# Attention and a gated feed-forward layer in one launch: low words on VectorE, leaky ReLU by one maximum, weights decoded during attention

## The chip, the cores and the metric

The kernel runs on one core of a Trainium2 chip. The metric is the device time of one execution in microseconds (us); the median of three runs before the change is 1651.07 us, the lowest 1649.44 and the highest 1653.55. The engines are TensorE (PE in the profile, its weight loads PEld), VectorE (DVE), ScalarE (ACT), GpSimd (POOL) and SyncE (SP), which issues the DMAs.

## The reference

First attention over 8 batches and 8 heads, 576 tokens, head width 64, in which scores more than `tau` under the row maximum are dropped; then a two-layer network with a leaky ReLU of one slope per hidden unit (512 to 2048 to 512, 4608 tokens). The inputs are float32 (the kernel reads the two weights as 64-bit words).

```python
scores = scale * np.matmul(q, k.transpose(0, 1, 3, 2))
thresh = np.max(scores, axis=-1, keepdims=True) - tau
scores = np.where(scores >= thresh, scores, -1000000000.0)
attn = np.exp(scores - max); attn = attn / (sum + 1e-09)
x = np.matmul(attn, v)            # then heads side by side: 4608 x 512
h = x @ w_in
g = np.maximum(h, 0.0) + alpha * np.minimum(h, 0.0)
return g @ w_out
```

## The kernel before

Matrix products are made in reduced float32 with operands split in a high word and a low word, `hi` rounded by ScalarE and `lo = value - hi` by a subtraction, and three matmuls per product: high by high, high by low, low by high.

The program has four stages. **Attention** runs over 32 pairs of heads, nine units each, one unit per cycle of the written order; functions are put at a cycle by `at_cycle(cycle, function)`, and each cycle issues what stands there on every engine in that order. A cycle is meant to last about 2.6 us. Between the units go the matmuls of the first 6 of 16 hidden blocks for all tokens, with the results kept in DRAM (`part`). TensorE makes scores (L424), VectorE the row maximum (L439) and the mask `p` (L459), ScalarE the exponential (L447).

**The left-over stage** finishes three groups of tokens (the jobs, tiles `phj`, `ptj`, `gj`, `accj`) by the same functions: `layer1_into` (L211), `prelu` (L229, L230), `split_g` (L238, L241), `layer2` (L247). Beside them `first_weights` decodes the first layer's ten other blocks, one every three cycles. A 64-bit word is taken apart by `Split64`: two operations on ScalarE (`size`: L134, L135), `clamp` (L138), then on VectorE `shift` (L141), `sign` (L146) and `power` (L151), then a product `rest` and a sum. `sums_at` makes from two blocks the seven weight operands of a fast 2x2 product with seven multiplications in place of eight, with high and low words (`wa`).

**The first product** has 30 units (six supers of 768 tokens by five pairs of blocks) of seven products each, each six matmuls of 384 columns (L1195), in the order `USE` = 1, 7, 2, 6, 4, 5, 3 into the banks X, W and Y. `after_a` (L1205 to L1227) makes the leaky ReLU: products 1, 7 and 6 are copied to SBUF by ScalarE (L1211); 2, 4 and 5 add the copy (VectorE, L1224), make the part under zero (L1225) and add the larger (L1226); product 3 takes VectorE (L1219), ScalarE (L1220) and POOL (L1221). `x_at` makes the next super's token operands, sums on POOL (`xt`, L1134 to L1144), `xh` on ScalarE (L842), `xl` on POOL (L845). The second layer's words are decoded in the same stage, one piece every 12 cycles (`word_at`; L826 and L830 are its sum and product).

**The second product** has nine groups of 512 tokens with seven products of 30 matmuls of 256 columns (L1353), in three parts with a cycle each. `gates_at` makes the operands: `gh` by ScalarE (L842), `gl` by VectorE for products 7 and 5 and by POOL for the other five (L845). Three pairs of buffers serve them in turn, so a product's `gh` waits until the product three before it is done. `after_b` adds the result into the output tile (L1369).

Of the kernel before, what the change touches and what calls it, by code (L numbers as in the profile page):

```python
# [79 lines left out]
def tile_masked_attention_moe(  # L80
# [31 lines left out]
    class Split64:  # L112
# [8 lines left out]
        def load(self):  # L121
            tag, bufs = self.raw_tag
            self.raw = self.pool.tile([P, DM], I64, tag=tag, name=f"wr{self.name}", bufs=bufs)
            nc.sync.dma_start(self.raw.rearrange("p (a b) -> p a b", a=self.a), self.src)

        def size(self):
# [4 lines left out]
            if pool is mem:  # L131
# [689 lines left out]
    def word_at(c, w, dst, load):  # L821


        def join():
            low, t = f(w.low), f(w.t)
            w.eng[2].tensor_tensor(dst, t, low, op=ALU.add)  # L826
# [6 lines left out]
        at_cycle(c, w.size)  # L833
# [5 lines left out]
        at_cycle(c + 6, join)  # L839
# [7 lines left out]
    def fetch_x(t0, n, c, lead, name):  # L847
# [24 lines left out]
        return st  # L872

    with tc.manual_schedule(engines=ENGINES) if ENGINES else ExitStack():
# [72 lines left out]
        def word_piece(io, fc):  # L947
            src = (src_i if io == "i" else src_o)(fc)
            return Split64(mem.ws, ("w0", 2), mem.ws, ("w1", 2), ENG2[(fc + (io == "o")) % 2], *src)

# [4 lines left out]

        def sums_at(c, pr):
# [97 lines left out]
        def second_layer(job, pool):  # L1054
            puts = []
            for o in range(0, job.n, P):
# [149 lines left out]
        def after_a(u, prod):  # L1206
            s, pr = divmod(u, NP)
            ph = bank[u, BANK[prod]][:, :H1]
            if prod in (1, 7, 6):
# [66 lines left out]
        def gates_at(s):  # L1276
# [179 lines left out]
```

## Time and profile before

| quantity | value |
|---|---|
| median of three runs | 1651.07 us |
| profiled execution | 1653.89 us |
| span of its trace | 1652.1 us |
| mean granted TensorE clock | 0.931 |
| TensorE matmuls busy | 1395.0 us (84%) |
| VectorE busy | 1228.5 us (74%) |
| ScalarE busy | 917.4 us (56%) |
| POOL busy | 884.8 us (54%) |

All rows come from one profiled execution. Busy time is that of the instructions that compute. [...] A wait is named by what released it last. The stages begin at 0, 836, 974 and 1294 us of the span, read from TensorE's instructions.

### The profile page before, as it was taken

Reading aid. Unit: us, or ns where it says so; the run is one execution under the profiler, and the core shown is the slowest. Engines: PE = TensorE matmul, PEld = TensorE weight load, DVE = VectorE, ACT = ScalarE, POOL = GpSimd, SP = SyncE. Lnnn points to the kernel's source line nnn. Section 1 sums busy time; section 2 is a strip of 40 time slices with the busy share of each in tenths; the row PEclk is TensorE's granted clock in tenths of the full one; section 3 lists DMA queues with packets and bytes.
Section 4 is the critical chain, followed back from the end, with each engine's and each line's share of the span. In section 5 each row is a group of like instructions: output and inputs, shape, how many; then the busy total and the mean of one; then the engine's idle time right before and its main releaser. Section 6 shows DMA issues by size and latency. Waiting matters only on the chain.

```text
span 1652.1 us, 26173 instructions
## 1 busy us (share of the span) xinstructions
PE 1395.0 (84%) x8998; PEld 1287.9 (78%) x8998; DVE 1228.5 (74%) x2203; ACT 917.4 (56%) x2019; POOL 884.8 (54%) x910
## 2 busy tenths in 40 slices
PE   6998999999999999999985577787787677777777
PEld 4667899998989999989975467786777677777777
DVE  7888889888898888888826788899889544444443
ACT  7888788888898888888733333332234222222222
POOL 4774656656576666666544445545655433333334
PEclk9998999999999999999988778999999788888889
DMA  7555454453554445545132333343324433333321
GB/s 221 162 147 138 108 142 132 138 159 110 144 143 129 139 126 147 139 133 149 45 95 74 102 106 112 134 145 118 107 84 166 154 125 114 118 121 115 104 67 52
DMA packets 143286, 205.08 MB, mean 124 GB/s; under 512 B 15696, under 2 KB 88688, under 8 KB 143152
## 3 DMA queue, kind: packets, MB, share of 16 engines
q1 hardware_dynamic: 143152, 203.39, 41.4%
q8 instruction: 72, 1.18, 0.3%
q14 instruction: 62, 0.51, 0.1%
HBM read 109.13 MB, written 52.05 MB: 98 GB/s over the span
## 4 chain that ended last, share of the span: by engine, by line
PE 57%; DVE 13%; issue 11%; ACT 8%; POOL 7%; DMA 4%; SPq 1%; ACTq 0%; POOLq 0%; DVEq 0%
PE av L571 10%; PE s L424 9%; PE acca L247 7%; PE pX L1353 7%; PE pha L211 7%; PE t L468 6%; POOL gl L845 4%; PE pX L1195 3%; PE pW L1353 3%; DVE ct L1225 3%; DMA wri<-in_moe_w_in_dram 2%; PE pY L1353 2%; DVE c L1224 2%; PE pW L1195 1%; ACT gh L842 1%
## 5 line engine op out<-in xcount | busy, mean ns | idle before, releaser
L439 DVE TENSOR_REDUCE nmx<-s 128x1 f32<-128x576 f32 x288 | 217.0, 754 | 79.0 <-PE s L424 75.4
L845 POOL TENSOR_TENSOR gl<-gr,gh 128x1280 fp32r<-128x1280 f32 x36 | 108.2, 3007 | 205.5 <-ACT gh L842 205.5
L1195 PE MATMUL pX<-xh,wa 128*128 128x384 f32 x480 | 147.9, 364 | 76.5 <-ACT c L1211 54.8
L459 DVE SCALAR_TENSOR_TENSOR p<-s,thr,p 128x576 f32<-128x576 f32 x256 | 206.9, 808 | 3.0 <-ACT thr L452 2.4
L447 ACT ACTIVATE p<-s,nmx 128x576 f32<-128x576 f32 x256 | 190.1, 742 | 5.9 <-DVE nmx L439 5.4
L424 PE MATMUL s<-kh,qst 128*128 128x288 f32 x640 | 145.0, 317 | 43.7 <-DVE p L459 28.2
L1353 PE MATMUL pX<-wb,gh 128*128 128x256 f32 x720 | 157.2, 319 | 20.7 <-ACT gh L842 20.7
L247 PE MATMUL acca<-wo,ga 128*128 128x512 f32 x540 | 169.1, 425 | 1.6 <-POOL ga L241 1.5
L1195 PEld LDWEIGHTS pX<-xh,wa 128*128 128x128 f32 x480 | 94.8, 202 | 88.2 <-ACT c L1211 61.3
L468 PE MATMUL t<-ident,p 128*128 128x128 f32 x1024 | 156.9, 277 | 0.0
L424 PEld LDWEIGHTS s<-kh,qst 128*128 128x128 f32 x640 | 101.7, 194 | 70.8 <-issue 39.3
L842 ACT ACTIVATE gh<-gr 128x1280 fp32r<-128x1280 f32 x45 | 55.9, 1262 | 179.0 <-issue 77.4
L1353 PEld LDWEIGHTS pX<-wb,gh 128*128 128x128 f32 x720 | 133.6, 227 | 23.9 <-ACT gh L842 23.9
L1353 PE MATMUL pX<-wb,gl 128*128 128x256 f32 x360 | 115.9, 322 | 39.5 <-POOL gl L845 39.5
L211 PE MATMUL pha<-xh,wi 128*128 128x256 f32 x720 | 146.5, 287 | 1.8 <-DVE tt L524 1.5
L424 PE MATMUL s<-kl,qst 128*128 128x288 f32 x640 | 135.1, 302 | 0.0
L468 PEld LDWEIGHTS t<-ident,p 128*128 128x128 f32 x1024 | 128.3, 143 | 0.2
L211 PEld LDWEIGHTS pha<-xh,wi 128*128 128x128 f32 x720 | 117.5, 190 | 7.0 <-DVE tt L524 2.4
L1353 PEld LDWEIGHTS pX<-wb,gl 128*128 128x128 f32 x360 | 82.0, 228 | 42.8 <-POOL gl L845 42.8
L571 PE MATMUL av<-eo,vst 128*128 128x322 f32 (+1 forms) x512 | 107.8, 334 | 0.0
L247 PEld LDWEIGHTS acca<-wo,ga 128*128 128x128 f32 x540 | 96.1, 194 | 13.9 <-POOL ga L241 2.0
L424 PEld LDWEIGHTS s<-kl,qst 128*128 128x128 f32 x640 | 104.1, 194 | 0.0
(201 smaller groups left out, 4079.9 us busy)
## 6 DMA issues: line engine op xcount, KB each, us to landing
gd<-c SPq DMA_DIRECT2D x90, 192.0 KB
gr<-gd SPq DMA_DIRECT2D x24, 640.0 KB
kr<-in_k_dram SPq DMA_DIRECT2D x31, 320.0 KB
rb<-rvd SPq DMA_DIRECT2D x64, 144.0 KB
xs<-xa SPq DMA_DIRECT2D x32, 288.0 KB
pin<-part SPq DMA_DIRECT2D x18, 512.0 KB
out_dram<-pin SPq DMA_DIRECT2D x18, 512.0 KB
vr<-in_v_dram SPq DMA_DIRECT2D x28, 320.0 KB
```

Of the source, the lines that this page charges most:

```text
L211: nc.tensor.matmul(ph[:, :n], w[:, c, :], xx[:, c, :n], start=(c == 0 and ti == 0), stop=(c == NCC - 1 and ti == 2),)
L247: nc.tensor.matmul(acc[:m, :], gg[:, g, o : o + m], w, start=(first and ti == 0), stop=(last and ti == 2))
L424: nc.tensor.matmul(ps[:, h, :288], w, kk[:, a + h * 288 : a + (h + 1) * 288], start=(ki == 0 and i == 0), stop=(ki == 1 and i == n - 1),)
L439: nc.vector.tensor_reduce(self.nmx[:, j : j + 1], self.S[u][0][:, :, :288], axis=AX.XY, op=ALU.max, negate=True)
L447: nc.scalar.activation(pj, ps[:, :, :288], AF.Exp, bias=nmx[:, j : j + 1], scale=1.0)
L459: nc.vector.scalar_tensor_tensor(pj, ps[:, :, :288], thr[:, j : j + 1], pj, op0=ALU.is_ge, op1=ALU.mult, accum_out=self.sm[:, c : c + 1])
L468: nc.tensor.transpose(tb[:, c, :], pt[:, j, j * D + c * P : j * D + (c + 1) * P], ident)
L571: nc.tensor.matmul(pa[:m, :n], w, x, start=(part == 0 and c == 0), stop=(part == z.parts[-1] and c == NKC))
L842: nc.scalar.activation(dst, src, AF.Copy)
L845: eng.tensor_tensor(dst, src, f(hi), op=ALU.subtract)
L1195: nc.tensor.matmul(ph[:, :H1], a, x[:, c], start=(fresh and c == 0 and ti == 0), stop=(c == 1 and ti == 2), skip_group_check=not fresh,)
L1353: nc.tensor.matmul(acc[:, tb * H2 : (tb + 1) * H2], g[:, pr, tb * P : (tb + 1) * P], w, start=(fresh and n == 0 and ti == 0), stop=(n == l ...
```

## The change

Three parts. **One:** the ten blocks' words of the first layer are decoded in attention, from cycle 62 on, one piece every 20 cycles, with clamp, product and sum on POOL, shift, sign and power on VectorE; the float32 result goes to DRAM (`wid`) and is read back after attention, so that `first_weights` holds only reads and sums, one pair every six cycles. **Two:** the leaky ReLU is one maximum: where alpha is at most 1 it is max(h, alpha h), and otherwise minus the maximum of -h and -alpha h; `signs` makes per hidden unit `turn` (1 or -1) and the products with it, the second layer's weights carry `turn`, and ScalarE's copies scale by it. The sum goes to PSUM (product 5 to a bank of its own, Z), ScalarE copies it to SBUF one cycle later, and one VectorE operation two cycles later makes the maximum. POOL's sum for product 3 goes. The second layer's words are decoded one piece every 14 cycles. **Three:** all `gl` of the second product are on VectorE.

```diff
+EW0, EW = 62, 20
+    def signs():
+        ts = nc.vector.tensor_scalar
+        ts(turn_sb, alpha_sb, 1.0, 2.0, op0=ALU.is_le, op1=ALU.mult)
+        ts(turn_sb, turn_sb, -1.0, None, op0=ALU.add)
+        ts(tiny_sb, turn_sb, 2.0**-52, None, op0=ALU.mult)
+        nc.vector.tensor_tensor(slope_sb, turn_sb, alpha_sb, op=ALU.mult)
+    wid = [dram.tile([P, DM], F32, name=f"wid{fc}") for fc in fcs2]
...
+    def early_word(n, c):
+        fc = fcs2[n]
+        w = Split64(mem, ("wx", 1), mem, ("wxt", 1), "ppp", *src_i(fc))
+        def done(w):
+            nc.gpsimd.tensor_tensor(f(w.t), f(w.t), f(w.low), op=ALU.add)
+            nc.sync.dma_start(wid[n], f(w.t))
+        word_at(c, w, c - 5, done)
...
+    at_cycle(6, signs)
+    for n_ in range(NJ):
+        early_word(n_, EW0 + EW * n_)
...
         def first_weights(c0, step):
-            for n, fc in enumerate(fcs2):
-                w = word_piece("i", fc)
-                c = c0 + step * n
-                at_cycle(c + 6, start_w32, fc)
-                word_at(c, w, None, c - 3)
...
+            for pr in range(NP):
+                c = c0 + step * pr
+                for r in range(2):
+                    at_cycle(max(i, c - 6), fetch_w32, 2 * pr + r)
+                sums_at(c, pr)
...
-        first_weights(i + 4, 3)
+        first_weights(i + 4, 6)
...
-                nc.scalar.activation(t, ph, AF.Copy)
+                nc.scalar.activation(t, ph, AF.Copy, scale=turn_sb[:, fc : fc + 1])
                 return
...
+            def larger(g, whole, slope):
+                stt(g, whole, slope[:, col], g, op0=ALU.mult, op1=ALU.max)
+                nc.sync.dma_start(gd[2 * s + k][r, pr], g)
             if of is None:
-                nc.vector.tensor_scalar(t, ph, 0.0, al, op0=ALU.min, op1=ALU.mult)
-                nc.scalar.activation(g, ph, AF.Relu)
-                nc.gpsimd.tensor_tensor(g, g, t, op=ALU.add)
+                copy(g, ph, scale=turn_sb[:, col])
+                at_cycle(i + 1, larger, g, ph, slope_sb)
             else:
                 g = sv.pop((u, of))
-                nc.vector.tensor_tensor(g, ph, g, op=ALU.add)
-                nc.vector.tensor_scalar(t, g, 0.0, al, op0=ALU.min, op1=ALU.mult)
-                nc.vector.scalar_tensor_tensor(g, g, 0.0, t, op0=ALU.max, op1=ALU.add)
+                whole = ph
+                if prod == 5:
+                    whole = ps_3.tile([P, 512], F32, tag="Z", name=f"pZ{u}")[:, :H1]
+                stt(whole, ph, turn_sb[:, col], g, op0=ALU.mult, op1=ALU.add)
+                at_cycle(i + 1, copy, g, whole)
+                at_cycle(i + 2, larger, g, whole, alpha_sb)
...
+            w = Split64(mem.ws, ("w0", 3), mem.ws, ("w1", 2), "ppp", *src_o(fc))
+            def done(w):
+                dst = wo32[:, n // 2, n % 2]
+                nc.vector.scalar_tensor_tensor(
+                    dst, f(w.t), turn_sb[:, fc : fc + 1], f(w.low), op0=ALU.mult, op1=ALU.add
+                )
+            word_at(c, w, c - 4, done, fc)
...
-            c = begin + 8 + 12 * n
+            late_word(n, begin + 8 + 14 * n)
...
-                split_lo(nc.vector if n in (7, 5) else nc.gpsimd, gop[s, n][1], st[src(n)], gop[s, n][0])
+                split_lo(nc.vector, gop[s, n][1], st[src(n)], gop[s, n][0])
```

On VectorE, in the first product, seven products of one unit: `c` are the tiles with the saved copies, `ct` temporary ones, `pX`, `pY`, `pW` PSUM banks. Before:

```order
L1224 TENSOR_TENSOR c_12_14008<-pY_14023,c_12_14008 128x384
L1225 TENSOR_SCALAR ct_12_14040<-c_12_14008,alpha_sb 128x384
L1226 SCALAR_TENSOR_TENSOR c_12_14008<-c_12_14008,ct_12_14040 128x384
L1219 TENSOR_SCALAR ct_11_14051<-pX_13900,alpha_sb 128x384
L1224 TENSOR_TENSOR c_12_14065<-pW_14010,c_12_14065 128x384
L1225 TENSOR_SCALAR ct_12_14074<-c_12_14065,alpha_sb 128x384
L1226 SCALAR_TENSOR_TENSOR c_12_14065<-c_12_14065,ct_12_14074 128x384
L1224 TENSOR_TENSOR c_12_14031<-pX_13978,c_12_14031 128x384
L1225 TENSOR_SCALAR ct_12_14094<-c_12_14031,alpha_sb 128x384
L1226 SCALAR_TENSOR_TENSOR c_12_14031<-c_12_14031,ct_12_14094 128x384
```

After:

```order
L1253 SCALAR_TENSOR_TENSOR pZ_13995<-pX_13882,turn_sb,c_11_13920 128x384
L1241 SCALAR_TENSOR_TENSOR c_11_13920<-pZ_13995,alpha_sb,c_11_13920 128x384
L1253 SCALAR_TENSOR_TENSOR pY_13997<-pY_13997,turn_sb,c_12_13982 128x384
L1241 SCALAR_TENSOR_TENSOR c_12_13982<-pY_13997,alpha_sb,c_12_13982 128x384
L1241 SCALAR_TENSOR_TENSOR cr_14022<-pX_13882,slope_sb,cr_14022 128x384
L1253 SCALAR_TENSOR_TENSOR pW_13985<-pW_13985,turn_sb,c_12_14035 128x384
L1241 SCALAR_TENSOR_TENSOR c_12_14035<-pW_13985,alpha_sb,c_12_14035 128x384
L1253 SCALAR_TENSOR_TENSOR pZ_14065<-pX_13956,turn_sb,c_12_14004 128x384
```

Three operations per product with two of them on SBUF alone have become two, both with a PSUM operand, and each maximum stands a product later than its sum.

On POOL, at a boundary of two supers: `xt` and `xr` are sums of token tiles, `xl` low words, `wo` and `wto` the second layer's words. Before:

```order
L1221 TENSOR_TENSOR cr_14131<-cr_14131,ct_12_14130 128x384
L1134 TENSOR_TENSOR xt_7_14167<-xr_11_13999,xr_01_14002 128x768
L845 TENSOR_TENSOR xl_1_14165<-xr_00_13997,xh_1_14164 128x768
L826 TENSOR_TENSOR wo_12979<-wto_14106,wro_14063 128x512
L845 TENSOR_TENSOR xl_7_14194<-xt_7_14167,xh_7_14193 128x768
L1141 TENSOR_TENSOR xt_6_14208<-xt_7_14167,xr_00_13997 128x768
L845 TENSOR_TENSOR xl_2_14206<-xr_10_14005,xh_2_14205 128x768
L1144 TENSOR_TENSOR xt_4_14224<-xr_10_14005,xt_6_14208 128x768
L1221 TENSOR_TENSOR cr_14227<-cr_14227,ct_13_14226 128x384
L845 TENSOR_TENSOR xl_6_14239<-xt_6_14208,xh_6_14238 128x768
```

After:

```order
L144 TENSOR_SCALAR wto_14074<-wto_14074 128x512
L1152 TENSOR_TENSOR xt_7_14131<-xr_11_13973,xr_01_13976 128x768
L843 TENSOR_TENSOR wro_14031<-wro_14031 128x512
L868 TENSOR_TENSOR xl_1_14129<-xr_00_13971,xh_1_14128 128x768
L868 TENSOR_TENSOR xl_7_14158<-xt_7_14131,xh_7_14157 128x768
L1159 TENSOR_TENSOR xt_6_14173<-xt_7_14131,xr_00_13971 128x768
L868 TENSOR_TENSOR xl_2_14171<-xr_10_13979,xh_2_14170 128x768
L1162 TENSOR_TENSOR xt_4_14185<-xr_10_13979,xt_6_14173 128x768
L868 TENSOR_TENSOR xl_6_14197<-xt_6_14173,xh_6_14196 128x768
L1156 TENSOR_TENSOR xr_01_13976<-xr_01_13976,xr_00_13971 128x768
```

The sums `cr` are gone; a clamp (`wto`, L144) and a product of words (`wro`, L843) stand there in place of the sum `wo`, and the order of the token operands is the same.

On VectorE, in the second product, some of one token group: `gt` and `gr` are sums of gates, `gl` the low words, `pin` the output tiles. Before:

```order
L845 TENSOR_TENSOR gl_5_16614<-gr_10_16190,gh_5_16613 128x1280
L1306 TENSOR_TENSOR gt_7_16627<-gr_00_16442,gr_10_16460 128x1280
L1369 TENSOR_TENSOR pin_1_16285<-pW_16444,pin_1_16285 128x2x256
L845 TENSOR_TENSOR gl_7_16652<-gt_7_16627,gh_7_16651 128x1280
L1369 TENSOR_TENSOR pin_0_16551<-pX_16638,pin_0_16551 128x2x256
L1317 TENSOR_TENSOR gr_01_16207<-gr_01_16207,gt_6_16474 128x1280
L1369 TENSOR_TENSOR pin_1_16285<-pX_16370,pin_1_16285 128x2x256
L1309 TENSOR_TENSOR gt_6_16743<-gr_11_16487,gt_7_16627 128x1280
L1369 TENSOR_TENSOR pin_1_16553<-pW_16713,pin_1_16553 128x2x256
L1369 TENSOR_TENSOR pin_0_16551<-pY_16759,pin_0_16551 128x2x256
L1369 TENSOR_TENSOR pin_0_16283<-pX_16370,pin_0_16283 128x2x256
```

After:

```order
L868 TENSOR_TENSOR gl_1_16759<-gr_00_16622,gh_1_16758 128x1280
L1407 TENSOR_TENSOR pin_1_16465<-pX_16550,pin_1_16465 128x2x256
L868 TENSOR_TENSOR gl_5_16796<-gr_10_16372,gh_5_16795 128x1280
L1344 TENSOR_TENSOR gt_7_16809<-gr_00_16622,gr_10_16641 128x1280
L1407 TENSOR_TENSOR pin_1_16465<-pW_16625,pin_1_16465 128x2x256
L868 TENSOR_TENSOR gl_7_16834<-gt_7_16809,gh_7_16833 128x1280
L1407 TENSOR_TENSOR pin_0_16733<-pX_16820,pin_0_16733 128x2x256
L1355 TENSOR_TENSOR gr_01_16388<-gr_01_16388,gt_6_16655 128x1280
L868 TENSOR_TENSOR gl_2_16869<-gr_01_16657,gh_2_16868 128x1280
L1407 TENSOR_TENSOR pin_1_16465<-pX_16550,pin_1_16465 128x2x256
L868 TENSOR_TENSOR gl_3_16908<-gr_01_16388,gh_3_16907 128x1280
```

Between the sums into `pin` four low words stand (1, 5, 7 and 2, then 3) where there were two.

On VectorE, in attention, one piece of words (`wti`, `wri`), which before the change has no row there:

```order
L147 TENSOR_SCALAR wti_6637<-wti_6637 128x512
L445 TENSOR_REDUCE nmx_4_6750<-s_4_6712 128x1
L465 SCALAR_TENSOR_TENSOR p_1_6665,sm_6527<-s_3_6669,thr_2_6663,p_1_6665 128x576
L530 TENSOR_TENSOR e_120<-t_2_6723,e_119 128x4x128
L152 SCALAR_TENSOR_TENSOR wti_6637<-wri_6438,wti_6637 128x512
L445 TENSOR_REDUCE nmx_5_6801<-s_5_6757 128x1
L465 SCALAR_TENSOR_TENSOR p_t,sm_6527<-s_4_6712,thr_4_6751,p_t 128x576
L530 TENSOR_TENSOR tt_124<-tk_1_6768,tt_123 128x128
L530 TENSOR_TENSOR eo_118<-t_3_6763,eo_117 128x4x128
L157 TENSOR_SCALAR wri_6438<-wti_6637 128x512
```

The three operations stand between row maxima (`nmx`, L445) and masks (`p`, L465), a cycle apart.

## Rows read from the trace of the kernel before

**Rows 1.** Windows: length; busy us (count) PE, PEld, DVE, ACT, POOL; clock; DMA share; GB/s.
```profile
200.00:836.00 636.00, 621.17 (x4477) 587.27 (x4477) 549.78 (x1215) 533.30 (x1273) 398.97 (x500) 0.99 0.47 129
836.00:974.00 138.00, 83.88 (x414) 68.66 (x412) 86.27 (x137) 46.14 (x107) 62.85 (x68) 0.80 0.30 92
974.00:1294.00 320.00, 249.34 (x1272) 237.94 (x1273) 281.16 (x393) 103.58 (x210) 167.22 (x112) 0.91 0.38 125
1294.00:1652.10 358.10, 271.54 (x1862) 261.37 (x1860) 144.18 (x114) 74.57 (x63) 132.24 (x46) 0.87 0.34 107
```

**Rows 2.** Waits, attention, TensorE: us in total, times, longest.
```profile
PE s L424 <- DVE p L459: 11.6, 10, 1.6
```

**Rows 3.** Lines, 836 to 974, VectorE: busy us, mean ns | idle before.
```profile
L146 DVE SCALAR_TENSOR_TENSOR wti<-wri,wti 128x512 int32<-128x512 int32 x10 | 9.4, 937 | 0.0
L141 DVE TENSOR_SCALAR wti<-wti 128x512 int32<-128x512 int32 x10 | 8.5, 848 | 0.0
L151 DVE TENSOR_SCALAR wri<-wti 128x512 int32<-128x512 int32 x10 | 5.2, 521 | 0.1
```

**Rows 4.** Lines by form, POOL: the cast, whole span; the sum of words, 974 to 1294.
```profile
L240 POOL CAST ga<-pta 128x256 fp32r<-128x256 f32 x87 | 34.5, 396 | 2.5
L826 POOL TENSOR_TENSOR wo<-wto,wro 128x512 f32<-128x512 f32 x5 | 6.7, 1332 | 8.4 <-DVE wro L830 8.4
```

**Rows 5.** Waits, 836 to 974.
```profile
ACT wti L134 <- DMA wri<-in_moe_w_in_dram: 50.0, 9, 6.8
PE phj L211 <- DVE ptj L230: 23.5, 3, 11.9
PE accj L247 <- ACT gj L238: 15.0, 4, 7.0
```

**Rows 6.** Chain of waits, attention: start, us, matmuls in a row.
```profile
801.87 1.43 PE pha L211 x12
830.54 2.75 PE acca L247 x12
```

**Rows 7.** Single lines, VectorE: ns min/median/max; last row: lines, 974 to 1294.
```profile
L1224 DVE TENSOR_TENSOR c<-pW,c x30: 544/558/560, 978.5 to 1287.3; 128x384 f32<-128x384 f32 x30
L1225 DVE TENSOR_SCALAR ct<-c,alpha_sb x90: 419/422/2128, 974.8 to 1289.8; 128x384 f32<-128x384 f32 x90
L1226 DVE SCALAR_TENSOR_TENSOR c<-c,ct x90: 557/559/2110, 975.3 to 1290.8; 128x384 f32<-128x384 f32 x90
L1219 DVE TENSOR_SCALAR ct<-pX,alpha_sb x30: 603/612/619, 985.4 to 1294.2; 128x384 f32<-128x384 f32 x30
L1225 DVE TENSOR_SCALAR ct<-c,alpha_sb 128x384 f32<-128x384 f32 x90 | 72.3, 804 | 5.3
```

**Rows 8.** Chain of waits, first product; windows of line 1195 (PE, PEld).
```profile
1205.05 1.04 PE pW L1195 x6
974.00:1294.00 320.00, 244.86 (x1242) 232.94 (x1242) 0.91 0.38 125
```

**Rows 9.** Waits, 974 to 1294.
```profile
PE pX L1195 <- ACT c L1211: 54.8, 18, 8.2
PE pX L1195 <- DVE c L1224: 21.7, 14, 3.7
```

**Rows 10.** Timeline, POOL, at a boundary of supers: start, us.
```profile
1234.23 1.98 POOL L845 TENSOR_TENSOR xl<-xr,xh 128x768 fp32r<-128x768 f32 x1
```

**Rows 11.** Timeline, TensorE, one token group of the second product [idle before].
```profile
1492.12 0.58 PE L1353 MATMUL pW<-wb,gl 128*128 128x256 f32 x1 [1.02 <-DVE gl L845]
1505.11 0.38 PE L1353 MATMUL pX<-wb,gl 128*128 128x256 f32 x1 [2.48 <-POOL gl L845]
```

**Rows 12.** Waits, 1294 to 1652.
```profile
PE pX L1353 <- POOL gl L845: 39.5, 16, 2.5
```

**Rows 13.** Lines by form, 1294 to 1652.
```profile
L845 POOL TENSOR_TENSOR gl<-gr,gh 128x1280 fp32r<-128x1280 f32 x35 | 105.0, 3003 | 204.4 <-ACT gh L842 204.4
L845 DVE TENSOR_TENSOR gl<-gt,gh 128x1280 fp32r<-128x1280 f32 x8 | 11.9, 1492 | 52.9 <-ACT gh L842 52.9
```

More of the change, by code (lines that the diff above doesn't have):

```diff
@@ L106, in tile_masked_attention_moe @@
     alpha_sb = const.tile([P, NF], F32, name="alpha_sb")
+    turn_sb = const.tile([P, NF], F32, name="turn_sb")
+    tiny_sb = const.tile([P, NF], F32, name="tiny_sb")
+    slope_sb = const.tile([P, NF], F32, name="slope_sb")
     xs = [dram.tile([NCC, P, S], F32, name=f"xs{b}") for b in range(B)]
@@ L122, in load, with size @@
             tag, bufs = self.raw_tag
-            self.raw = self.pool.tile([P, DM], I64, tag=tag, name=f"wr{self.name}", bufs=bufs)
+            self.raw = (mem.mp1 if self.pool is mem else self.pool).tile([P, DM], I64, tag=tag, name=f"wr{self.name}", bufs=bufs)
             nc.sync.dma_start(self.raw.rearrange("p (a b) -> p a b", a=self.a), self.src)
-        def size(self):
+        def size(self, scale=2.0**-52):
             words = self.raw.bitcast(I32).rearrange("p (n two) -> p n two", two=2)
@@ L130, in size @@
             pool = self.temp_pool
-            if pool is mem:
+            if pool is mem and self.pool is mem:
+                pool = mem.mp1
+            elif pool is mem:
                 pool, tag, bufs = (mem.mp1, "g", GB) if mem.mp1 else (spool, "wt", 4)
@@ L134, in size @@
             nc.scalar.activation(f(self.t), f(self.high), AF.Abs)
-            nc.scalar.activation(f(self.low), self.low.bitcast(U32), AF.Copy, scale=2.0**-52)
+            nc.scalar.activation(f(self.low), self.low.bitcast(U32), AF.Copy, scale=scale)
         def clamp(self):
-            self.eng[0].tensor_scalar(f(self.t), f(self.t), WORD_LO, WORD_HI, op0=ALU.max, op1=ALU.min)
+            self.eng[0].tensor_scalar(f(self.t), f(self.t), WORD_HI, WORD_LO, op0=ALU.min, op1=ALU.max)
         def shift(self):
@@ L819, in tile_masked_attention_moe, with word_at @@
     gd = [dram.tile([2, NP, P, H1], F32, name=f"gd{h}") for h in range(NT // H1)]
[L821 to L826, printed above, removed]
+    def signs():
[5 more added lines that the diff above has]
+    wid = [dram.tile([P, DM], F32, name=f"wid{fc}") for fc in fcs2]
+    def word_at(c, w, load, done, fc=None):
         def rest():
@@ L832, in word_at @@
         at_cycle(load, w.load)
-        at_cycle(c, w.size)
+        at_cycle(c, w.size, *(() if fc is None else (tiny_sb[:, fc : fc + 1],)))
         at_cycle(c + 1, w.clamp)
@@ L838, in word_at @@
         at_cycle(c + 5, rest)
-        at_cycle(c + 6, join)
+        at_cycle(c + 6, done, w)
+    def early_word(n, c):
[5 more added lines that the diff above has]
+        word_at(c, w, c - 5, done)
     def split_hi(dst, src):
@@ L945, in tile_masked_attention_moe, with fetch_w32 @@
         wsum = {}
-        def word_piece(io, fc):
-            src = (src_i if io == "i" else src_o)(fc)
-            return Split64(mem.ws, ("w0", 2), mem.ws, ("w1", 2), ENG2[(fc + (io == "o")) % 2], *src)
         w32 = {}
-        def start_w32(fc):
-            w32[fc] = mem.ws.tile([P, DM], F32, tag="w32", name=f"w32_{fc}", bufs=4)
+        def fetch_w32(n):
+            fc = fcs2[n]
+            if n % 2 == 0:
+                w32[n // 2] = mem.ws.tile([P, 2, DM], F32, tag="w0", name=f"w32_{n // 2}", bufs=3)
+            nc.sync.dma_start(w32[n // 2][:, n % 2], wid[n])
         def sums_at(c, pr):
@@ L959, in sums_at @@
             m = DM // 2
-            blk = lambda r, k: w32[fcs2[2 * pr + r]][:, k * m : (k + 1) * m]
+            blk = lambda r, k: w32[pr][:, r, k * m : (k + 1) * m]
             def temps():
@@ L1063, in second_layer @@
                 cycle()
-                po = pool.tile([P, DM], F32, tag="po", name=f"po{job.name}_{o}", bufs=1 if pool is mem.mp1 else 2)
+                po = pool.tile([P, DM], F32, tag="po" if pool is mem.mp1 else "w1", name=f"po{job.name}_{o}", bufs=1 if pool is mem.mp1 else 2)
                 def put(o=o, m=m, acc=acc, po=po):
@@ L1210, in after_a @@
                 t = sv[u, prod] = mem.br.tile([P, H1], F32, tag=f"c{prod}", name=f"c{prod}_{u}", bufs=2)
-                nc.scalar.activation(t, ph, AF.Copy)
+                fc = fcs2[2 * pr + (0 if prod == 1 else 1)]
+                nc.scalar.activation(t, ph, AF.Copy, scale=turn_sb[:, fc : fc + 1])
                 return
@@ L1214, in after_a, with copy @@
             fc = fcs2[2 * pr + r]
-            al = alpha_sb[:, fc : fc + 1]
-            t = mem.br.tile([P, H1], F32, tag="ct", name=f"ct{prod}_{u}", bufs=2)
+            col = slice(fc, fc + 1)
+            stt = nc.vector.scalar_tensor_tensor
+            def copy(g, whole, **scale):
+                nc.scalar.activation(g, whole, AF.Copy, **scale)
+            def larger(g, whole, slope):
+                stt(g, whole, slope[:, col], g, op0=ALU.mult, op1=ALU.max)
+                nc.sync.dma_start(gd[2 * s + k][r, pr], g)
@@ new lines, in after_a, with late_word @@
+                stt(whole, ph, turn_sb[:, col], g, op0=ALU.mult, op1=ALU.add)
+                at_cycle(i + 1, copy, g, whole)
+                at_cycle(i + 2, larger, g, whole, alpha_sb)
+        wo32 = mem.br.tile([P, NP, 2, DM], F32, name="wo32")
+        def late_word(n, c):
+            fc = fcs2[n]
+            w = Split64(mem.ws, ("w0", 3), mem.ws, ("w1", 2), "ppp", *src_o(fc))
[5 more added lines that the diff above has]
+            word_at(c, w, c - 4, done, fc)
```

11 lines of the change are left out of this document (1 added, 10 removed).

## The prediction, made before the changed kernel had run

> **What bounds the kernel now.** I read the trace in four steps. First the busy time by stage [rows 1]. In attention (200 to 836 us) TensorE is busy 621 of 636 us, VectorE 550: TensorE is the bound, and of its few waits the largest is for VectorE's softmax mask, 11.6 us in ten waits [rows 2]. After attention nothing is full: TensorE works 84 of 138 us in the left-over stage (836 to 974), 249 of 320 in the first product (974 to 1294), 272 of 358 in the second. The granted clock is there 0.80, 0.91 and 0.87, against 0.99 in attention, so a wait is paid twice: once as idle time and once as matmuls that run at the lower level after it. Second the waits by stage: which engine does TensorE wait for [rows 5, 9, 12]. Third the price of each operation [rows 3, 4, 7, 13]. Fourth TensorE's pace where it waits for nothing [rows 6, 8], which says how far a stage can fall.
>
> **The decoding of the first layer's weights, in attention.** Ten pieces of 512 words, one per 20 cycles. VectorE gets shift, sign and power: 0.85 + 0.94 + 0.52 = 2.3 us per piece [rows 3], 23 us in all, into 86 us that it has free in that stretch [rows 1]. POOL gets clamp, product and sum. Product and sum are the size of L826, 1.33 us [rows 4]. No row shows POOL's clamp (two scalars, 512 columns): the cast of 256 columns takes 0.40 [rows 4], by columns 0.8; the upper bound taken is that of a two-input operation, 1.33. So 3.5 us per piece, 35 us into POOL's 237 free ones. ScalarE's two operations per piece are those that it did later; its 533 of 636 us bear them. Ten writes and ten reads of 256 KB are added on SP's queue; the share of the DMA engines is 0.47 there, and loads of q and k and the moves stand behind them some cycles ahead of their use, so I cost them at nothing; uncovered it would be the length of one POOL step, 1.3 us, each time: 13. What is paid is VectorE's order: the shift now waits for POOL's clamp, and behind it on VectorE stand the row maxima and masks for which TensorE waits. A wait on POOL would be paid where POOL is over a cycle late. 30 operations of 0.8 us are 24; I take a third of them as paid, nearer to the ten mask waits of now than to the 23: 8 us. The bounds are 0 (all in VectorE's gaps) and 40 (23 us, and half of POOL's 35 as waits). The four small sign operations come once and cost under 1 us; taken in.
>
> **The left-over stage (836 to 974).** Decoding leaves it, and only reads, sums and splits stay beside three jobs of the first algorithm. TensorE waits 23.5 us for VectorE's leaky ReLU of a job and 15.0 for the cast behind it [rows 5], 38.5 in all; both come late because VectorE and ScalarE work off the decode in the same order, and ScalarE stands 50 us for raw words [rows 5]. I leave 6 of the 38.5: the chain behind a block itself. TensorE's 83.9 us at 0.80 are some 67 at full clock (an estimate; the jobs proper are 216 / 12 x 1.43 + 108 / 12 x 2.75 = 50.5 by [rows 6]). So 138 = 84 + 54 idle becomes 67 + 54 - 32 = 89, a gain of 48. Bounds: 25 (two thirds of the waits, no clock), 58 (ten us more of the idle time go).
>
> **The first product (974 to 1294).** Per unit of seven products the three leaky ReLUs were 3 x (0.55 + 0.42 + 0.56) and 0.61 on VectorE, 5.2 us undisturbed, but the two forms with SBUF operands alone go to 2.13 and 2.11 [rows 7] while the form with a PSUM operand never passes 0.56. L1225's mean is 0.80, twice its median. TensorE's pace is 7 x 1.04 = 7.28 us per unit [rows 8]; a super of five units is 36.4, and 320 us for 30 units is 53. Now there are seven operations with a PSUM operand per unit, 7 x 0.56 = 3.9, and all but the last reads of SBUF are gone; POOL loses 30 sums of `cr`. The stage is 1242 / 6 = 207 products [rows 8] x 1.04 = 215, plus waits 76.5 (54.8 on ScalarE's copy, 21.7 on VectorE's sum) [rows 9], plus 249 - 215 = 34 of half clock. Which waits stay? At a boundary of two supers POOL makes eight operands in a row at 1.98 us [rows 10], 15.9 us, begun 5.3 ahead of the unit: product 4's comes some 4.1 late, five times, 20.5; the clamp and product of the second layer's words stand in that burst at two boundaries, 4 more; VectorE's decode operations wait for POOL's clamp, 5; the last unit, 5. So 34.5 of 76.5, and half clock in proportion, 15. That gives 265: a gain of 55. ScalarE gets 90 + copies in place of relu, at most 90 x 0.56 = 50, and is at 154 of 265. Bounds: 20 (the burst holds everything as before, only VectorE's 21.7 go), 75 (no wait but the boundary's 20.5, and clock to 0.96).
>
> [...]
>
> **The second product (1294 to 1652).** The `gl` of five products in seven go from POOL, 3.00 us, to VectorE, 1.49 where POOL is quiet [rows 13]; POOL then has nothing there. TensorE waits 2.48 for a `gl` of POOL and 1.02 for one of VectorE [rows 11], since three products in a row share a buffer. Sixteen waits of 39.5 us [rows 12] become 16 x 1.02 = 16.3: 23, and 2 for the clock. VectorE's queue per group: 7 x 1.5 + 4 x 1.5 + 7 x 0.7 = 21 of some 40 us. Gain 25; bounds 15 (each `gl` stands behind a sum half of the time, 0.7 x 16) and 35 (clock to 0.95).
>
> **Sum.** +8 - 48 - 55 - 25 = -120 on a span of 1652.1: 1532. The profiled execution lasted 1653.9, 1.8 above its span and 2.8 above the median of 1651.07; so 1653.9 - 120 - 2.8 = 1531.
>
> **Rivals.**
> 1. The burst rules the first product: the waits are POOL's operands reaching ScalarE's queue late, which the change leaves. For it: 54.8 of 76.5 us are on ScalarE's copy, and ScalarE's `xh` stands behind POOL's `xt`. Against it: the units between boundaries are slow too (53 against 36.4). It keeps 32 of the 55: 1563. Chance 0.13.
> 2. Attention pays: each of VectorE's 30 decode operations waits out a POOL operation, 1.3 us mean, and TensorE with it at the full: 30 x 0.85 + 10 x 1 = 35 instead of 8. For it: 2.13 and 2.11 [rows 7]. Against: only ten waits on the mask now. 1558. Chance 0.13.
> 3. Attention hides all (8), the boundary is met by the freed POOL (15), and the clock comes back whole (12): 1496. Chance 0.15.
> 4. It doesn't do what it says: the waits of the left-over stage are the jobs' own chain, and decode is beside it. For it: the three waits for `ptj` reach 11.9 us, longer than any decode operation. Against it: the cast `gj`, with the same chain, is late by 3.7 us in the mean, four times only [rows 5], so it isn't late in every block. 1531 + 30 = 1561. Chance 0.03.
> 5. The slower side: POOL's clamp. With no row of its size it may be of a slow kind; ten in attention stand in POOL's order ahead of the casts that feed the second layer and of the moves, ten more in the first product at the burst. Spread over the ten in attention, 120 us are gone at 12 us each; at 15 us each it is 1681. The cast's 0.40 [rows 4] speaks against it. Chance 0.03.
>
> **How the numbers follow.** The forecast's own range is 1508 to 1555, chance 0.53. Cases 1, 2 and 4 lie at 1558 to 1563, case 3 at 1496; with the bounds (all the good ones would be 1483, all the bad ones 1631) the range for eight in ten is 1486 to 1580. Under 0.3%, 5 us, is no change that a measurement tells. Only case 5 reaches it: slower 0.03, same 0.01, faster 0.96.
>
> **What would show it.** Attention: the mask wait's sum [rows 2] at 20 or below. Left-over stage: the waits for `ptj` and `gj` under 10 us, clock over 0.85. First product: the new operations with PSUM operands flat near 0.56, TensorE's wait on ScalarE's copies under 40, at the boundaries of supers only. Second: no wait for POOL, each for a `gl` near 1.0. Wrong it would be if POOL's clamp took over 2 us, if the stretch to the end of attention grew by over 20, or if the first product stayed over 295.

## The result, and the profile after

The changed kernel takes 1534.7 us in the median of four executions, the kernel before 1652.26; the ratio is 0.928, with a 95% interval of 0.925 to 0.931. The forecast was 1531. The execution that was profiled first took 4497 us, its matmuls of 512 columns 1179 ns in the mean (425 in the kernel before) at a recorded clock of 1.00, for a reason that the record does not show; it is left out of the ratio, and the other three took 1529 to 1536. The trace below is of another run of the same kernel, span 1527.8 us (four executions, 1527.8 to 1541.6, ratio 0.929, 0.924 to 0.933).

To compare stages I cut both traces at the same instructions: the last matmul of attention's values, the first matmul of the first product and the first of the second. The cuts of [rows 1] lie 1 us before, 12 and 6 us behind those. First the windows of the kernel before by these cuts, with the columns of [rows 1]; the first window begins at 200 us:

```profile
200.00:837.30 637.30, 622.47 (x4486) 588.57 (x4486) 549.78 (x1215) 533.90 (x1274) 399.51 (x500) 0.99 0.46 129
837.30:962.40 125.10, 78.65 (x387) 64.33 (x387) 78.78 (x131) 39.71 (x98) 55.27 (x63) 0.80 0.31 96
962.40:1288.30 325.90, 247.57 (x1256) 235.27 (x1256) 283.30 (x391) 108.68 (x216) 173.53 (x114) 0.91 0.37 123
1288.30:1652.10 363.80, 277.24 (x1897) 267.06 (x1896) 149.52 (x123) 75.29 (x65) 132.97 (x47) 0.87 0.34 107
```

Then those of the kernel after:

```profile
200.00:853.60 653.60, 626.54 (x4469) 585.85 (x4468) 567.28 (x1237) 541.09 (x1287) 427.40 (x526) 0.99 0.50 137
853.60:927.20 73.60, 65.82 (x387) 57.89 (x387) 41.74 (x78) 30.06 (x79) 46.89 (x60) 0.95 0.42 134
927.20:1220.20 293.00, 234.96 (x1256) 224.89 (x1256) 180.89 (x288) 157.17 (x304) 140.49 (x97) 0.94 0.42 135
1220.20:1527.80 307.60, 245.43 (x1897) 234.00 (x1896) 178.31 (x164) 76.87 (x67) 2.25 (x2) 0.98 0.41 127
```

| stage | before | after | difference | forecast |
|---|---|---|---|---|
| attention, to its last matmul | 837.3 | 853.6 | +16.3 | +8 |
| left-over stage | 125.1 | 73.6 | -51.5 | -48 |
| first product | 325.9 | 293.0 | -32.9 | -55 |
| second product | 363.8 | 307.6 | -56.2 | -25 |
| span | 1652.1 | 1527.8 | -124.3 | -120 |

The sum is right, and of its four terms only that of the left-over stage is. TensorE's busy time is over half of the gain in the second product: it falls from 277 to 245 us with the same matmuls, while the granted clock rises from 0.87 to 0.98.

TensorE's waits after the change (us in total, times, longest), in attention, where [rows 2] had 11.6 and the wait for `pra` was 0.2:

```profile
PE s L430 <- DVE p L465: 15.7, 18, 2.0
PE pha L217 <- ACT pra L230: 4.5, 7, 1.6
```

In the left-over stage, where the waits for `ptj` and `gj` of [rows 5] are gone and this is the largest:

```profile
PE phj L217 <- ACT xhj L887: 4.4, 2, 3.4
```

In the first product, against [rows 9]:

```profile
PE pX L1213 <- DVE pZ L1253: 34.6, 13, 9.9
PE pX L1213 <- ACT c L1230: 19.2, 11, 6.5
PE pW L1213 <- ACT c L1230: 4.2, 3, 2.5
```

In the second, against [rows 12]:

```profile
PE pX L1391 <- ACT gh L865: 19.9, 16, 1.3
PE pX L1391 <- DVE gl L868: 18.8, 22, 1.0
PE pW L1391 <- ACT gh L865: 10.3, 8, 1.3
PE pW L1391 <- DVE gl L868: 8.2, 8, 1.0
```

No wait for POOL is left there; what is left is 1.24 to 1.29 us for a high word and mostly 1.02 for a low one. Single instructions (ns min/median/max), the sum into PSUM, the maximum, the shift of a word, and POOL's clamp of 512 columns:

```profile
L1253 DVE SCALAR_TENSOR_TENSOR pW<-pW,turn_sb,c x30: 612/623/626, 941.3 to 1219.0; 128x384 f32<-128x384 f32 x30
...
L1241 DVE SCALAR_TENSOR_TENSOR c<-pW,alpha_sb,c x30: 604/618/620, 943.2 to 1221.0; 128x384 f32<-128x384 f32 x30
```

```profile
L147 DVE TENSOR_SCALAR wto<-wto x16: 417/686/2051, 63.3 to 1112.5; 128x512 int32<-128x512 int32 x16
```

```profile
L144 POOL TENSOR_SCALAR wto<-wto x10: 607/615/645, 943.8 to 1111.8; 128x512 f32<-128x512 f32 x10
```

The operations with a PSUM operand are flat, at 0.62 us where the forecast had 0.56 ([rows 7] has 0.61 for L1219, which reads PSUM too); the shift, on SBUF alone, still goes from 0.42 to 2.05. POOL's clamp takes 0.62, under the 0.8 that I took. In the second product the low words cost what [rows 13] said:

```profile
L868 DVE TENSOR_TENSOR gl<-gr,gh 128x1280 fp32r<-128x1280 f32 x44 | 65.4, 1487 | 72.6 <-ACT gh L865 72.6
```

### The profile page after: what moved, and what is told of

It reads as the page before. It is cut to its first block, busy times and chain, and to the rows that moved or that the text cites. A ratio compares the mean times of both kernels' runs of the same rounds, so it can differ in the third digit from the quotient of the medians.

```text
span 4495.6 us, 26143 instructions
## 1 busy us (share of the span) xinstructions
PE 4440.6 (99%) x8998; PEld 3506.9 (78%) x8998; DVE 1155.7 (26%) x2122; ACT 982.2 (22%) x2109; POOL 728.0 (16%) x875
## 4 chain that ended last, share of the span: by engine, by line
PE 98%; DVE 1%; ACT 1%; SPq 0%; issue 0%; DMA 0%; POOL 0%; ACTq 0%; POOLq 0%; DVEq 0%
PE av L577 15%; PE s L430 13%; PE t L474 11%; PE acca L253 10%; PE pX L1213 10%; PE pha L217 10%; PE pX L1391 10%; PE pW L1213 5%; PE pW L1391 5%; PE pY L1213 2%; PE pY L1391 2%; PE accj L253 2%; PE phj L217 2%; PE tk L490 1%; DVE gl L868 1%; ACT gh L865 1%
## 5 line engine op out<-in xcount | busy, mean ns | idle before, releaser
L445 DVE TENSOR_REDUCE nmx<-s 128x1 f32<-128x576 f32 x288 | 218.1, 757 | 1236.8 <-PE s L430 1236.5
L253 PE MATMUL acca<-wo,ga 128*128 128x512 f32 x540 | 533.3, 1179 | 0.0
L474 PE MATMUL t<-ident,p 128*128 128x128 f32 x1024 | 491.9, 692 | 0.0
L217 PE MATMUL pha<-xh,wi 128*128 128x256 f32 x720 | 423.6, 690 | 0.0
L1391 PE MATMUL pX<-wb,gh 128*128 128x256 f32 x720 | 382.0, 652 | 15.1 <-ACT gh L865 15.1
L430 PE MATMUL s<-kh,qst 128*128 128x288 f32 x640 | 383.4, 751 | 13.0 <-DVE qst L351 11.2
L1213 PE MATMUL pX<-xh,wa 128*128 128x384 f32 x480 | 378.3, 890 | 0.0
L1391 PEld LDWEIGHTS pX<-wb,gh 128*128 128x128 f32 x720 | 359.8, 589 | 23.4 <-ACT gh L865 23.1
L430 PE MATMUL s<-kl,qst 128*128 128x288 f32 x640 | 373.4, 735 | 0.0
L577 PE MATMUL av<-eo,vst 128*128 128x322 f32 (+1 forms) x512 | 336.5, 868 | 0.0
L577 PEld LDWEIGHTS av<-eo,vst 128*128 128x128 f32 (+1 forms) x512 | 200.5, 404 | 83.4 <-issue 56.2
L217 PE MATMUL pha<-xl,wi 128*128 128x256 f32 x360 | 245.1, 681 | 0.0
L465 DVE SCALAR_TENSOR_TENSOR p<-s,thr,p 128x576 f32<-128x576 f32 x256 | 206.9, 808 | 11.7 <-ACT thr L458 10.9
```

The costliest lines, as they stand in the source:

```text
L217: nc.tensor.matmul(ph[:, :n], w[:, c, :], xx[:, c, :n], start=(c == 0 and ti == 0), stop=(c == NCC - 1 and ti == 2),)
L253: nc.tensor.matmul(acc[:m, :], gg[:, g, o : o + m], w, start=(first and ti == 0), stop=(last and ti == 2))
L430: nc.tensor.matmul(ps[:, h, :288], w, kk[:, a + h * 288 : a + (h + 1) * 288], start=(ki == 0 and i == 0), stop=(ki == 1 and i == n - 1),)
L445: nc.vector.tensor_reduce(self.nmx[:, j : j + 1], self.S[u][0][:, :, :288], axis=AX.XY, op=ALU.max, negate=True)
L465: nc.vector.scalar_tensor_tensor(pj, ps[:, :, :288], thr[:, j : j + 1], pj, op0=ALU.is_ge, op1=ALU.mult, accum_out=self.sm[:, c : c + 1])
L474: nc.tensor.transpose(tb[:, c, :], pt[:, j, j * D + c * P : j * D + (c + 1) * P], ident)
```

## The experiments

Ratios are to the kernel before, with 95% intervals.

**after_again**: the changed kernel, for the trace above.

> The changed kernel once more, for a trace of an undisturbed execution. The prediction's theory: of the 117 us gained, attention pays 8 (to 844), the left-over stage takes about 90 us, the first product about 265, the second about 333. Rival 1 (POOL's operands at the boundaries of supers rule the first product): the first product stays near 297 and another stage gave more. Rival 2 (attention pays): the first stage ends near 871 and the products gave more.

Measured 1534.6. Attention paid 16 (the theory said 8, rival 2 said 35). The first product took 293, near the 297 of rival 1, and the second 308.

**early_alone**: part one alone (two places of the edit; the rest is as in the kernel before).

```diff
+    for n_ in range(NJ):
+        early_word(n_, EW0 + EW * n_)
...
-        first_weights(i + 4, 3)
+        first_weights(i + 4, 6)
```

> Part one alone: the first layer's words decoded in attention; leaky ReLU, the second layer's words and the second product as before. The prediction's theory: attention 8 longer, the left-over stage 48 shorter, 1612 us. Rival 2 (VectorE's decode operations each wait out POOL and TensorE pays in full): 35 and 48, 1639. Rival 4 (the left-over stage is bound by the jobs' own chain): 1642 or more, with the waits for ptj and gj as before.

Measured 1620.4, ratio 0.981 (0.978 to 0.984), 8 over the theory. Attention ends at 855.2 (+17.9), the left-over stage takes 73.9 (-51.2), the products are unchanged at 325.6 and 365.8. Rival 4 falls: the jobs' own chain does not bind that stage.

**leaky_alone**: part two alone (the leaky ReLU of a product that adds a saved copy).

```diff
-                nc.vector.tensor_tensor(g, ph, g, op=ALU.add)
-                nc.vector.tensor_scalar(t, g, 0.0, al, op0=ALU.min, op1=ALU.mult)
-                nc.vector.scalar_tensor_tensor(g, g, 0.0, t, op0=ALU.max, op1=ALU.add)
+                stt(whole, ph, turn_sb[:, col], g, op0=ALU.mult, op1=ALU.add)
+                at_cycle(i + 1, copy, g, whole)
+                at_cycle(i + 2, larger, g, whole, alpha_sb)
```

> Part two alone: leaky ReLU by one maximum with the sum in PSUM, sign in the weights, the second layer's words with clamp and product on POOL; first layer's words and the second product as before. The prediction's theory: the first product 55 shorter, 1597 us. Rival 1 (POOL's operands at the boundaries of supers rule it): 23 shorter, 1629, with TensorE's waits on ScalarE's copies left at 40 or more.

Measured 1598.8, ratio 0.967 (0.964 to 0.970): the total of the theory, but not for its reason. The first product gave 28 (325.9 to 298.0), and 23 came from the left-over stage (125.1 to 101.8), whose work had not been touched. But part two also brings three buffers for raw words where there were two; raw3 tests it.

**gl_alone**: part three alone.

```diff
-                split_lo(nc.vector if n in (7, 5) else nc.gpsimd, gop[s, n][1], ...
+                split_lo(nc.vector, gop[s, n][1], ...
```

> Part three alone: all low words of the second product on VectorE, the rest as before. The prediction's theory: the second product 25 shorter, 1627 us, each wait for a low word near 1.0 us. Rival: VectorE's order makes each low word wait behind a sum into the output half of the time, 15 shorter, 1637.

Measured 1594.2, ratio 0.965 (0.962 to 0.968): 58 faster, over twice the theory. The window of the second product (TensorE busy, weight loads, VectorE, ScalarE, POOL, clock):

```profile
1283.30:1596.40 313.10, 250.85 (x1897) 239.67 (x1895) 179.91 (x167) 76.11 (x65) 4.86 (x3) 0.96 0.40 125
```

Idle time of TensorE falls from 363.8 - 277.2 = 86.6 to 62.3, which is the 24 that the prediction worked out; another 26 are the same matmuls at a higher clock (0.96 in this window, 0.87 before). Some 5 us more of this trace lie in the stages ahead, which the edit does not touch, and stay unexplained.

The three parts alone give 32 + 53 + 58 = 143 us, together 118. The next run looks for the difference.

**raw3**: the kernel before with a third buffer for raw words; to make room, the job's result takes the other words' tag.

```diff
-            return Split64(mem.ws, ("w0", 2), mem.ws, ("w1", 2), ...
+            return Split64(mem.ws, ("w0", 3), mem.ws, ("w1", 2), ...
...
-                po = pool.tile([P, DM], F32, tag="po", ...
+                po = pool.tile([P, DM], F32, tag="po" if pool is mem.mp1 else "w1", ...
```

> The kernel before with three buffers for raw words in place of two (the tile of the job's result takes the tag w1 for it), nothing else. Theory: part two alone shortened the left-over stage from 125 to 102 us only by this third buffer, since ScalarE stands for raw words: 23 shorter, 1629 us. Rival: the clamp and the product on POOL did it: 1650.

Measured 1629.4, ratio 0.985 (0.983 to 0.987), on the number. The left-over stage takes 101.7 us, as in leaky_alone. Its waits, to be read against [rows 5]:

```profile
PE phj L211 <- DVE ptj L230: 9.6, 2, 6.5
PE accj L247 <- ACT gj L238: 8.6, 4, 3.6
...
ACT wti L134 <- DMA wri<-in_moe_w_in_dram: 4.2, 1, 4.2
```

ScalarE no longer stands for raw words (4.2 us for 50.0), and the waits for `ptj` and `gj` fall from 38.5 to 18.2. This saving is in part one, which takes the words out of the stage, and in part two, and can be had once: 143 - 24 = 119.

**no_vector**: attention with ScalarE's and POOL's part of the words; it leaves out VectorE's.

```diff
+        for part in ("shift", "sign", "power"):
+            setattr(w, part, lambda: None)
```

> The changed kernel without VectorE's shift, sign and power for the first layer's words in attention (so these weights are not what the reference has); ScalarE's two and POOL's three operations stay. Theory of the prediction: attention pays 16 us for VectorE's operations between masks, so attention ends near 841 in place of 853.6. Rival: it is ScalarE's two operations ahead of a relu: 850 or more.

One run, 1519.1. Attention ends at 838.1, 15.5 earlier than with the three operations, and the waits on the mask are back at 11.7 us; the window first, then the waits:

```profile
200.00:838.10 638.10, 620.08 (x4469) 583.20 (x4468) 549.13 (x1210) 541.12 (x1287) 425.36 (x526) 1.00 0.51 140
```

```profile
PE s L430 <- DVE p L465: 11.7, 12, 1.6
PE pha L217 <- ACT pra L230: 1.6, 5, 0.4
```

So VectorE's 30 operations, with what they wait for, cost 15.5 of the 16.3 us, and most of the wait on ScalarE's `pra`. ScalarE's and POOL's 50 cost nothing that can be told: in the five traces without words in attention (before, leaky_alone, gl_alone, raw3, both_late) it ends at 834.7 to 838.4, in the five with all of them (after_again, early_alone, words_between, turns, both) at 852.7 to 855.2.

**words_between**: the second layer's words between POOL's bursts.

```diff
-            late_word(n, begin + 8 + 14 * n)
+            late_word(n, begin + (8, 15, 45, 52, 80, 87, 115, 122, 150, 157)[n])
```

> The changed kernel with the second layer's words put between the bursts of POOL at the boundaries of supers, two pieces per super. Theory: the waits left in the first product (two of 9.9 us and smaller ones) are VectorE's final sum of a word waiting for POOL's product behind the token operands: the first product 293 to about 262, 1504 us. Rival 1 of the prediction (POOL's burst itself makes operands late): the first product stays at 288 or more, 1530.

Measured 1502.4, ratio 0.908 (0.906 to 0.910). Window and TensorE's waits in the first product:

```profile
926.60:1192.40 265.80, 234.76 (x1255) 225.57 (x1254) 171.85 (x288) 157.02 (x305) 138.64 (x97) 0.95 0.46 149
```

```profile
PE pX L1213 <- ACT c L1230: 18.2, 9, 6.5
PE pX L1213 <- DVE pZ L1253: 10.2, 7, 1.8
...
PE pY L1213 <- POOL xl L868: 0.3, 1, 0.3
```

The place is seen in the changed kernel, where one of the two waits of 9.9 us ends (start, us, engine, instruction, idle before). POOL:

```profile
1024.73 1.80 POOL L868 TENSOR_TENSOR xl<-xt,xh 128x768 fp32r<-128x768 f32 x1
1026.49 1.03 POOL L843 TENSOR_TENSOR wro<-wro 128x512 f32<-128x512 f32 x1
```

VectorE:

```profile
1016.87 2.03 DVE L147 TENSOR_SCALAR wto<-wto 128x512 int32<-128x512 int32 x1 [1.13 <-POOL wto L144]
1018.93 2.22 DVE L152 SCALAR_TENSOR_TENSOR wto<-wro,wto 128x512 int32<-128x512 int32 x1
...
1023.03 0.61 DVE L1253 SCALAR_TENSOR_TENSOR pW<-pW,turn_sb,c 128x384 f32<-128x384 f32 x1
1027.56 2.27 DVE L1265 SCALAR_TENSOR_TENSOR wo<-wto,turn_sb,wro 128x512 f32<-128x512 f32 x1 [3.92 <-POOL wro L843]
1029.76 0.61 DVE L1241 SCALAR_TENSOR_TENSOR c<-pW,alpha_sb,c 128x384 f32<-128x384 f32 x1
1030.29 0.61 DVE L1253 SCALAR_TENSOR_TENSOR pZ<-pX,turn_sb,c 128x384 f32<-128x384 f32 x1
```

TensorE:

```profile
1030.95 0.69 PE L1213 MATMUL pX<-xh,wa 128*128 128x384 f32 x1 [9.90 <-DVE pZ L1253]
```

The word's product (L843) stands behind the token operands on POOL. VectorE waits 3.92 us for it at the word's last sum (L1265), behind which stand the maximum of product 4 and the sum of product 5, which frees the bank that TensorE's next product needs. The word's shift (L147) and sign (L152), 2.03 and 2.22 us, came just before.

What is left at a boundary with the words out of the way is still POOL's burst, seen through two other engines. From words_between, ScalarE, then VectorE, then TensorE:

```profile
976.69 0.85 ACT L865 ACTIVATE xh<-xt 128x768 fp32r<-128x768 f32 x1 [2.27 <-POOL xt L1162]
977.91 0.48 ACT L1238 ACTIVATE c<-pW 128x384 f32<-128x384 f32 x1
```

```profile
978.42 0.62 DVE L1241 SCALAR_TENSOR_TENSOR c<-pW,alpha_sb,c 128x384 f32<-128x384 f32 x1 [3.35 <-ACT c L1238]
978.96 0.62 DVE L1253 SCALAR_TENSOR_TENSOR pZ<-pX,turn_sb,c 128x384 f32<-128x384 f32 x1
```

```profile
979.63 0.45 PE L1213 MATMUL pX<-xh,wa 128*128 128x384 f32 x1 [1.76 <-DVE pZ L1253]
```

ScalarE waits for POOL's sum for product 4, its copy comes late, with it VectorE's maximum and the sum behind it, and TensorE waits 1.76 us; the wait is put down to VectorE, which ended last. The same chain stands at all five boundaries; with some 0.7 us just before, for a copy behind another operand, they cost TensorE 12.3 us. The rest of its waits there is 6.5 in the first unit and some 10 in the last super.

**turns**: buffers of the second product by the order in time.

```diff
-                r = 7 * s + use.index(n)
+                r = [p for p in steps if p[0] >= NA].index((NA + s, n))
```

> The changed kernel with the three pairs of buffers of the second product given out in the order of time in place of the order within a group, so that no two products in a row share one. Theory: the 57 us of waits left there (19.9 and 10.3 on the high word, 18.8 and 8.2 on the low word) are this sharing: all go but the first group's, 1480 us. Rival: the high words' place in ScalarE's and VectorE's order makes them late whatever the buffer: half of it stays, 1507.

Measured 1457.8, ratio 0.881 (0.879 to 0.883): 77 faster than the changed kernel where 54 were expected. In the changed kernel the buffers go round within a group, but two groups interleave in time: three times per group a product has the buffers of the product just before it (products 4 and then 1 of the next group, 5 and then 7, 2 and then 3), and not of the product three before. With the edit TensorE has no wait left in the stage:

```profile
1223.90:1456.70 232.80, 228.33 (x1897) 228.12 (x1896) 182.65 (x164) 79.94 (x67) 2.25 (x2) 0.99 0.53 168
```

It is busy 228 of 233 us at a clock of 0.99. I had counted the idle 57 us and again not the busy time, which fell by 17 us (245.4 to 228.3) while the clock went from 0.98 to 0.99; of the 17 the clock is some 2.5 by my estimate (245 x 0.01), and what makes the rest was not shown.

**both**: the last two edits together.

> The changed kernel with both edits that helped: the second layer's words between POOL's bursts, and the buffers of the second product given out in the order of time. They lie in different stages, so the gains add: 1534 - 32 - 77 = 1425 us. Rival: the second product's first group starts on operands that the words' later places delay, and 10 of it are lost: 1435.

Measured 1430.1 (1428.1 to 1432.9), ratio 0.867 (0.865 to 0.869). The median lies between the two theories; the stages (74, 266, 233) are those of the single runs, so nothing shows what the rival named.

**both_late**: the same with the first layer's words after attention, from three buffers of raw words.

> The same with the first layer's words decoded after attention again, from three buffers of raw words, each sum of a word as in the kernel before. Theory: part one is worth only what it saves beyond the third buffer, 28 us of the left-over stage, less the 16 that attention pays: 11 longer than both, 1436 us. Rival: attention's 16 us are dearer than the rest of the decode, equal or below both, 1425 or less.

Measured 1438.5, ratio 0.871 (0.870 to 0.873), near the theory's 1436. Beside the third buffer, part one is worth 8 us.

## Why the prediction was right, and where its steps were not

The total was right by luck in part. Attention cost 8 more than forecast and the first product gave 22 less, the second gave 31 more and the left-over stage 4: the errors cancel to 4 us.

- **Attention** (+8, measured +16.3). The mechanism held: it is VectorE's three operations, and nothing of POOL's or ScalarE's that can be told (no_vector). The size was off: I took a third of 24 us as paid, two thirds were. The shift takes 0.38 to 1.82 us there, and TensorE's waits are more (18 on the mask for 10) rather than much longer. Of the 16.3 us, 12 are idle time of TensorE and 4 busy time.
- **Left-over stage** (-48, measured -51.5). Right in sum and in clock (0.80 to 0.95). The cause was named as the queue that decode shares with the jobs; raw3 shows that 23 of it was the supply of raw words, a row that I quoted [rows 5] and did not price apart.
- **First product** (-55, measured -32.9; the sign of being wrong, 295, was missed by 2). The step that failed is the price of the second layer's words: "4 more" for their clamp and product in POOL's burst and "5" for VectorE waiting behind the clamp; moving them gave 27 (293.0 to 265.8). The burst itself holds product 4 up as the prediction said, but by 12.3 us over five boundaries and not 20.5 (words_between). The stage comes to my 265 only with the words moved. That VectorE's leaky ReLU is no longer slowed by POOL was right: the new operations are flat (0.60 to 0.63 us in all 210), and 283 us of VectorE in the stage became 181, of which some 16 are the words' clamp and product that went to POOL.
- **Second product** (-25, measured -56.2). The waits were right in size, 24 us of idle time, though not in their reason: it is not three products in a row that share a buffer (turns). "And 2 for the clock" is the step that failed: it was 32. In the kernel before, two waits close together (1.29 us at 1502.13, then 2.48 [rows 11]) are followed by some 3.5 us of matmuls at the lower level: the granted clock is 0.50 from 1506 to 1509 us and 1.00 from 1510 to 1513. In the first stretch a `gl` matmul takes 0.41 us, in the second 0.28:

```profile
1502.13 0.50 PE L1353 MATMUL pX<-wb,gh 128*128 128x256 f32 x2 [1.29 <-ACT gh L842]
...
1507.28 0.41 PE L1353 MATMUL pX<-wb,gl 128*128 128x256 f32 x1
...
1511.69 0.28 PE L1353 MATMUL pX<-wb,gl 128*128 128x256 f32 x1
```

After the change the pair of waits is 1.24 and 1.02 us, and a `gl` matmul behind it takes 0.28 us at once:

```profile
1368.12 0.39 PE L1391 MATMUL pX<-wb,gl 128*128 128x256 f32 x1 [1.02 <-DVE gl L868]
...
1368.58 0.28 PE L1391 MATMUL pX<-wb,gl 128*128 128x256 f32 x1
```

The length of the pair alone does not decide it. Each group has a third pair, of 1.29 and 1.02 us, which the change leaves as it is. In the kernel before, matmuls at the lower level follow it too (behind the 1.02 of [rows 11], with a clock of 0.50 from 1493 to 1495 us); in the changed kernel they do not (0.41 us against 0.29):

```profile
1490.60 0.50 PE L1353 MATMUL pW<-wb,gh 128*128 128x256 f32 x2 [1.29 <-ACT gh L842]
...
1494.21 0.41 PE L1353 MATMUL pW<-wb,gl 128*128 128x256 f32 x1
```

```profile
1356.65 0.50 PE L1391 MATMUL pW<-wb,gh 128*128 128x256 f32 x2 [1.29 <-ACT gh L865]
1358.18 0.39 PE L1391 MATMUL pW<-wb,gl 128*128 128x256 f32 x1 [1.02 <-DVE gl L868]
...
1358.64 0.29 PE L1391 MATMUL pW<-wb,gl 128*128 128x256 f32 x1
```

A stretch of matmuls at the lower level stands behind 23 of the 24 pairs before, and behind 2 of the 24 after (at 1243.60 and 1265.02, pairs of 1.24 and 1.02); in gl_alone, with pairs as after the change, behind 5. So with the two long pairs of a group shortened, nearly the whole stage stays at full clock (0.98 in its window, 0.96 in gl_alone, 0.87 before), the untouched pairs included; what decides it at a single pair is open. I had priced the clock by the idle time saved.

What POOL's work beside it does to an operation of VectorE shows in the trace of the kernel before. L1225 and L1226 are on SBUF alone. Of the 90 of each, 50 and 62 take 0.42 and 0.56 us, and through all but one of these POOL is idle for three quarters of the time or more; the other 40 and 28 take 0.44 to 2.13 and 0.97 to 2.11 us, and POOL works through half or more of each. L1224, which reads PSUM, takes 0.54 to 0.56 us in all 90, with POOL at work through 43 of them. VectorE, then POOL:

```profile
1240.84 0.56 DVE L1224 TENSOR_TENSOR c<-pW,c 128x384 f32<-128x384 f32 x1 [0.27 <-ACT c L1211]
1241.43 2.12 DVE L1225 TENSOR_SCALAR ct<-c,alpha_sb 128x384 f32<-128x384 f32 x1
```

```profile
1240.50 1.00 POOL L1221 TENSOR_TENSOR cr<-cr,ct 128x384 f32<-128x384 f32 x1 [1.94 <-ACT cr L1220]
1241.47 1.86 POOL L845 TENSOR_TENSOR xl<-xr,xh 128x768 fp32r<-128x768 f32 x1
```

After the change the shift, on SBUF alone, goes from 0.42 to 2.05 us, the sum with a PSUM operand from 0.61 only to 0.63. By what means the one engine holds up the other, no run shows.

Rival 1 had the number of the first product (293 for its 297) and not the cause: words_between takes 27 us away with POOL's token operands in the same order, and what its mechanism still costs is the 12.3 us. Rival 2 is refuted by its size (16, not 35), 4 by early_alone, 5 by the clamp's 0.62 us. Rival 3's 1496 was not reached.

## What to carry to other kernels

Price a wait twice: the idle time, and the pace of the matmuls behind it as the trace shows it. When one part of a change gains time in a stage that it does not touch, look for what else came with it (here one more buffer). Where an engine that works in order waits for a helper, and the helper has a burst of other work, put the job away from the burst. Give buffers out in the order of use. These two edits gave 32 and 77 us, the change itself 118. And follow a wait back past the engine that ended last: the waits on VectorE at the boundaries began at POOL.

## What was not expected of the hardware

Operations of 384 columns that write PSUM from PSUM and SBUF take 0.62 us (0.61 to 0.63), one with an SBUF target and a PSUM operand the same (0.60 to 0.62), over 210 of them. POOL's operation with two scalars on 512 columns takes 0.62 us, half of its two-operand sum (L826, 1.31 in the kernel before). Waits of 1.3 and 1.0 us close together were followed by matmuls at the lower level in the kernel before (0.41 us for a `gl` matmul), where longer pairs stand beside them, and were not in the changed kernel (0.29), where none do.
